# A two-head state product on VectorE: one instruction with a masked decay in place of two half-height ones

## The chip, the core and the metric

The kernel runs on one core of a Trainium2 chip. The metric is the time of one execution on the device in microseconds; what is shown is the median of several runs. The engines are TensorE (PE in the profile; PEld is its loading of weights), VectorE (DVE), ScalarE (ACT), GpSimd (POOL), and SP, which issues most DMAs.

## What is computed

A recurrent attention with a state per head (4 batches, 8 heads, 768 steps, 40 channels a head) is followed by a two-layer network with a squared ReLU. Cut to what matters:

```
for t in range(S):
    y[:, :, t] = einsum('bhd,bhde->bhe', r_t, state)
    Sa = einsum('bhde,bhe->bhd', state, a_t)
    state = state * w_t[:, :, None, :] - einsum('bhd,bhe->bhde', Sa, b_t)
    state = state + einsum('bhd,bhe->bhde', v_t, k_t)
x = y with the heads of a token side by side          # 3072 x 320
out = relu(x @ w_in) ** 2 @ w_out                     # 3072 x 2048, then 3072 x 320
```

## The kernel before

The sequence is cut into 6 chunks of 128 tokens. In a chunk the recurrence is turned into matrix products, and only the state at the chunk's end goes on to the next chunk. A chunk of one of the 4 batches is a "batch" m of the code (24 of them), prepared by `add_prep`. Its 8 heads are 4 pairs; two pairs make a "step" (`add_step`, 48 steps, two per batch). In a pair, head s = 0 has partitions 0 to 63 and head s = 1 partitions 64 to 127, with 40 of the 64 filled.

In the preparation of a batch, ScalarE turns the decays w into logarithms and exponentials, GpSimd and VectorE make the scaled keys KB and cast the rest to bf16, and TensorE or a transposing DMA turns them. The cumulative decays of the chunk end in the tile GT (5 in a ring, line 151): 128 partitions, 4 pairs, 130 columns, of which column 0 is one and columns 1 to 128 are the decays (`e_gt`); column L = 128 is the decay over the whole chunk. Batch 0 is prepared in two parts of two pairs (`o.parts`, line 253), all others in one.

A step runs through: products ca and their masking CN (line 485, DVE); the matmuls P and two corrections (lines 494 to 509) with c between them (line 522, DVE); the transposition TB, which also turns the carried state (lines 546 and 552); the products ex and their masking EVX (line 571, DVE); the matmuls of line 582 (`kb_mm`) and, from chunk 1 on, those of line 590 (`z_mm`), which leave outputs and new state together in one PSUM bank: 168 columns a pair, 128 of outputs and 40 of state. From there `ys` (line 595) writes the outputs of the step and `uz` (line 599) the state, both multiplied by decays of GT on VectorE.

`uz(u)` is called twice a step in the first five chunks (40 steps, 80 instructions), once for each head u of both pairs. Its result goes into the tile UZ of the next chunk (2 in a ring, line 153): 128 partitions, 16 pairs, 128 columns, in which head 0 has the columns 0 to 39 of its 64 partitions and head 1 the columns 64 to 103 of its own. The other two blocks of a pair must be zero, since the matmul of line 494 contracts over all 128 partitions. They are zero because `blank` (line 195) zeroes each whole tile at the start, and `uz` never writes there.

The instructions of all engines are issued in one written-out order (`ORDER`, line 835, with the engine of each movable operation in `WAYS`): `add_step` only declares operations with their costs and needs, here `("UZ", st, u)` at line 649, and a planner assigns buffers and banks while it follows the order. Each engine works its own instructions off in that order. The two products of a step stand next to each other in some places and up to five microseconds apart in others, with either head first: steps 0, 1, 3, 2 begin with head 0, steps 4, 5, 7, 9 with head 1, steps 6 and 8 with head 0. The readers of the state are the transposes of line 552, four steps or more later, and the matmuls of line 494, eight steps later. The transposes of a step, the network's matmuls (lines 723 and 760) and the rest of the step's matmuls fill TensorE in between. In the network `hs` and `Gt` (lines 731 to 742) are spread over ScalarE, VectorE and GpSimd.

Of the kernel before, what the change touches and what calls it, by code (L numbers as in the profile page):

```python
# [8 lines left out]
BF16 = mybir.dt.bfloat16  # L9
I32 = mybir.dt.int32  # L10
ALU = mybir.AluOpType
# [7 lines left out]
def kernel(  # L19
# [12 lines left out]
    nc = tc.nc  # L32

    NB, NHH, T, D = r.shape
    L = 128
    NCH = T // L
    PB = NHH // 2
# [6 lines left out]
    LV = L + D  # L44
# [4 lines left out]
    gl = ctx.enter_context(tc.tile_pool(name="gl", bufs=1))  # L49
# [30 lines left out]
    def buf(ring, kind=None):  # L80
        b_ = Buf(ring, kind)
        if ring != "bank":
            row = rings.setdefault(ring, [])
            b_.n = len(row)
            row.append(b_)
        return b_
# [58 lines left out]
    MEX = gl.tile([128, 4, L], BF16, name="MEX")  # L145
    IDs = gl.tile([128, D], BF16, name="IDs")
    MCN = gl.tile([128, 2, 2, L], BF16, name="MCN")
    banks = [ps.tile([128, 512], FP32, name=f"bank{i}") for i in range(NBANK)]
    fixed = {}
    for ring, shape in (("KB", [128, 2, NHH, 64]), ("GA", [128, 2, NHH, 64]),  # L150
                        ("RV", [128, 2, NHH, 64]), ("GT", [128, PB, L + 2]),
                        ("EVX", [128, PB, 2, EV]), ("RVT", [128, 2, PB, L]),
                        ("UZ", [128, NP, 128])):
        fixed[ring] = [gl.tile(shape, BF16, name=f"{ring}{i}") for i in range(RING[ring])]
# [5 lines left out]
        out=UTI[:], in_=ones_f[:], pattern=[[1, 128]],  # L160
# [5 lines left out]
        out=IDb[:], in_=ones_b[:], pattern=[[1, 128]],  # L166
# [6 lines left out]
    for i in range(26):  # L173
# [3 lines left out]
        out=UTb[:], in_=ones_b[:], pattern=[[1, 128]],  # L177
# [4 lines left out]
        out=MEX[:], in_=MEX[:], pattern=[[0, 4], [1, L]],  # L182
# [3 lines left out]
    def blank(ring, i):  # L186
        t_ = fixed[ring][i]
        if ring in ("KB", "GA", "RV"):
            nc.vector.memset(t_[:, :, :, D:64], 0.0)
        elif ring == "GT":  # L190
            nc.gpsimd.memset(t_[:, :, 0:1], 1.0)
        elif ring == "EVX":
            nc.gpsimd.memset(t_[:, :, :, 2 * LV:EV], 0.0)
        elif ring == "UZ":
            nc.vector.memset(t_[:], 0.0)

    for i in range(2):
        for ring in ("KB", "GA", "RV"):
            blank(ring, i)
    for u, sg in ((0, 1.0), (1, -1.0)):  # L200
        nc.vector.tensor_scalar(out=MCN[:, :, u, :], in0=MEX[:, 0:2, :],
                                scalar1=sg, scalar2=None, op0=ALU.mult)
    for i in range(2):
        for ring in ("GT", "EVX"):
            blank(ring, i)
    later = {}
    for ring, a_, b_, eng, cost in (("KB", 2, 5, "DVE", 0.21), ("UZ", 1, 2, "DVE", 1.0),
                                    ("GT", 2, 5, "POOL", 0.05), ("EVX", 2, 5, "POOL", 0.2),
                                    ("UZ", 0, 1, "DVE", 1.0)):
        for i in range(a_, b_):  # L210
            rank = i - 1.5 if ring != "UZ" else (7.0, 0.5)[i]
            later[ring, i] = ("blank", ring, i)
            op(("blank", ring, i), eng, rank, cost, cost + 0.05, [], [],
               lambda ring=ring, i=i: blank(ring, i))
# [5 lines left out]
    def half(s):  # L220
        return slice(64 * s, 64 * s + 64)
# [23 lines left out]
    for m in range(NBC):  # L245
        o = Batch()
# [9 lines left out]
    def part(m, u):  # L256
        return u if m < SPLIT else 0

    def sb(b_, shape, dtype):
        if b_.tile is None:  # L260
            pool = natp if b_.ring[0] == "N" else rot
            b_.tile = pool.tile(shape, dtype, name=b_.ring, tag=b_.ring,
                                bufs=RING[b_.ring if b_.ring in RING else "N"])
        return b_.tile
# [184 lines left out]


    SU, MERGE = 4, 12
    CNb, TBb = [buf("CN") for _ in range(NS)], [buf("TB") for _ in range(NS)]
    c1b, x1b = ([buf(x) for _ in range(NS)] for x in ("c1", "x1"))
    Mcb, Ccb = ([buf(x) for _ in range(NCH)] for x in ("Mc", "Cc"))
    UZb, YSb = [None] + [buf("UZ") for _ in range(1, NCH)], [buf("YS") for _ in range(NCH)]
# [3 lines left out]
    def add_step(st):  # L459
        c, q = divmod(st, NQ)  # L460
        m, u_ = divmod(st, 2)
        o, j0, p2, p = bt[m], 2 * u_, slice(2 * q, 2 * q + 2), part(m, u_)
        EVX = o.EVX.tile[:, j0:j0 + 2]
        UZ = UZb[c].tile if c else None
# [5 lines left out]
        def quads(b_):  # L470
            return b_.tile[:].rearrange("p (i u t) -> p i u t", i=2, u=2)
# [11 lines left out]
        def cn(s):  # L483
            t_ = sb(CN_, [128, 2, 2, 2, L], BF16)
            nc.vector.tensor_tensor(out=t_[:, :, s], in0=quads(ca[s]), in1=MCN[:], op=ALU.mult)  # L485

# [88 lines left out]
        def uy():  # L575
            return uyb.tile[:, 0:2 * LV].rearrange("p (i x) -> p i x", i=2)
# [19 lines left out]
                                    in1=o.GT.tile[:, j0:j0 + 2, 0:L], op=ALU.mult)  # L596

        def uz(u):
            nc.vector.tensor_tensor(  # L599
                out=UZb[c + 1].tile[half(u), p2, 64 * u:64 * u + D], in0=uy()[half(u), :, L:LV],  # L600
                in1=o.GT.tile[half(u), j0:j0 + 2, L:L + 1].to_broadcast([64, 2, D]), op=ALU.mult)

        op(("ca", st), "PE", st, *pe(0.225), [("KBT", m, p), ("AT", m, p)], [o.KBT, o.AT] + ca,
           ca_mm, "R")
# [25 lines left out]
        n = 512 if carry else 256  # L630
# [16 lines left out]
        if c + 1 < NCH:  # L647
            for u in range(2):
                op(("UZ", st, u), "DVE", st + 4.05, 0.15, 0.234,
                   [last, ("GT", m, p)] + cleared("UZ", c + 1), [uyb, o.GT, UZb[c + 1]],  # L650
                   lambda u=u: uz(u))
# [437 lines left out]
```

## Time and profile before

| | |
|---|---|
| median of 3 runs | 274.46 us (272.98 to 274.72) |
| the profiled execution | 272.03 us |
| its span, first to last instruction | 270.3 us |
| granted TensorE clock over the span | 0.981 |
| busy: PE, DVE | 254.8 us, 241.0 us |
| busy: ACT, POOL | 206.8 us, 186.2 us |
| products of line 599 | 80, of 219 to 247 ns (median 236) |

The profile is one execution. An engine's busy time is the time that its instructions' records cover, and records on one engine overlap: the next instruction can start before the one ahead of it has ended. The chain is the work that ended last, followed back from the last instruction, at each step to what released it or to the instruction ahead of it on the same engine. In a group of instructions stand the line, the engine, the operation, the tiles written and read, the shapes and the count; then busy us and the mean ns of one; then the idle time of the engine in front of them and what ended it. In the timeline a row has the start, the time, the engine and the same names; in brackets stands the idle time ahead of it and its releaser.

### The profile page before, as it was taken

To read this page: it belongs to the slowest core of one execution; us is meant where nothing else is said; L and a number is where in the kernel's file an instruction comes from. 1 tells how busy PE (TensorE), PEld (TensorE's weight loads), DVE (VectorE), ACT (ScalarE), POOL (GpSimd) and SP (SyncE) were. 2 spreads that over 40 slices of the span, in tenths; PEclk is the share of its full clock that TensorE was granted. 3 is DMA by queue.
4 is the path that set the end of the run, shared out by engine and by line. 5 is a ranking of instruction groups with operands and counts; after the bars stand their busy time and mean duration, and the time that the engine had idled before them with its cause. 6 is when DMAs were issued, how large, how long until landed. Compare 5 with 4: busy or idle time off the path is not lost.

```text
span 270.3 us, 10143 instructions
## 1 busy us (share of the span) xinstructions
PE 254.8 (94%) x3944; PEld 205.7 (76%) x3944; DVE 241.0 (89%) x564; ACT 206.8 (77%) x542; POOL 186.2 (69%) x313
## 2 busy tenths in 40 slices
PE   7885989799999999999999999999999999999994
PEld 6653668578888778778888778888888777778773
DVE  7785899999999999999999999999999888898382
ACT  3474778888999979888999878787888767966560
POOL 4396947896979797799978668786945574143360
PEclk9998589999999999999999999999999999999999
DMA  7999999997983995898897889998999978904002
GB/s 120 172 179 158 155 168 174 166 183 124 158 150 59 184 150 94 157 182 145 162 175 143 149 156 150 184 140 160 165 124 118 180 130 166 153 11 112 6 29 75
DMA packets 184034, 37.61 MB, mean 139 GB/s; under 512 B 178544, under 2 KB 183664, under 8 KB 183984
## 3 DMA queue, kind: packets, MB, share of 16 engines
q1 hardware_dynamic: 181328, 34.33, 75.6%
q0 software_dynamic: 2656, 2.62, 6.6%
q8 instruction: 31, 0.51, 0.8%
q14 instruction: 19, 0.16, 0.2%
HBM read 28.84 MB, written 3.93 MB: 121 GB/s over the span
## 4 chain that ended last, share of the span: by engine, by line
PE 62%; DVE 14%; DMA 6%; SPq 5%; ACT 4%; issue 4%; POOL 3%; DVEq 0%; POOLq 0%; ACTq 0%
PE bank L723 19%; PE bank L760 14%; PE bank L346 5%; SPq L272 5%; PE bank L582 5%; PE bank L477 4%; DVE CN L485 4%; PE bank L509 3%; PE bank L566 3%; DVE EVX L571 3%; PE bank L300 2%; PE bank L590 2%; DMA KBT<-KB 2%; DVE YS L595 2%; DMA NA<-in_a_dram 2%
## 5 line engine op out<-in xcount | busy, mean ns | idle before, releaser
L723 PE MATMUL bank<-YS,WIN 120*128 120x256 bf16 (+3 forms) x672 | 75.0, 257 | 0.3 <-DVE CN L485 0.3
L571 DVE TENSOR_TENSOR EVX<-bank,MEX 128x512 bf16<-128x512 f32 x96 | 63.8, 679 | 2.2 <-PE bank L566 1.7
L485 DVE TENSOR_TENSOR CN<-bank,MCN 128x512 bf16<-128x512 f32 x96 | 62.8, 679 | 2.0 <-PE bank L477 1.3
L723 PEld LDWEIGHTS <-WIN 120*128 120x128 bf16 (+1 forms) x672 | 54.6, 97 | 7.6 <-issue 0.4
L760 PE MATMUL bank<-WOUT,Gt 128*128 128x320 bf16 x384 | 58.6, 299 | 0.0
L742 POOL TENSOR_TENSOR Gt<-hs 128x512 bf16<-128x512 bf16 x38 | 39.6, 1044 | 26.6 <-ACT hs L731 14.5
L731 ACT ACTIVATE hs<-bank 128x512 bf16<-128x512 f32 x74 | 42.9, 596 | 8.2 <-PE bank L723 3.2
L760 PEld LDWEIGHTS <-Gt 128*128 128x128 bf16 x384 | 34.9, 97 | 12.4 <-issue 0.2
L534 ACT ACTIVATE junk<-CN 128x512 bf16<-128x512 bf16 x48 | 30.1, 628 | 1.5 <-DVE CN L485 1.0
L526 POOL TENSOR_TENSOR x<-Mc,c 128x160 f32<-128x160 bf16 x41 | 20.8, 510 | 13.5 <-DVE c L522 11.8
L331 POOL TENSOR_TENSOR KB<-NB,GI 128x320 bf16<-128x320 f32 (+1 forms) x22 | 18.8, 856 | 12.7 <-DMA NB<-in_b_dram 12.6
L530 POOL TENSOR_TENSOR Cc<-x,EVX 128x160 bf16<-128x160 f32 x46 | 23.3, 513 | 2.9 <-DVE EVX L236 1.4
L509 PEld LDWEIGHTS <-CN 128*128 128x128 bf16 x384 | 19.6, 97 | 5.8 <-issue 1.8
L582 PE MATMUL bank<-EVX,KB 128*64 128x168 bf16 x384 | 23.4, 245 | 0.1
L331 POOL TENSOR_TENSOR KB<-NK,GI 128x320 bf16<-128x320 f32 (+1 forms) x23 | 19.7, 858 | 5.1 <-ACT GI L321 2.7
L740 ACT ACTIVATE Gt<-hs 128x512 bf16<-128x512 bf16 x35 | 21.7, 632 | 1.2 <-DVE hs L733 1.0
L231 ACT ACTIVATE TB<-bank 128x512 bf16<-128x512 bf16 (+1 forms) x29 | 16.8, 578 | 7.2 <-PE bank L552 4.4
L477 PE MATMUL bank<-AT,KBT 64*128 64x128 bf16 x384 | 19.8, 222 | 2.1 <-ACT KBT L231 1.2
L595 DVE TENSOR_TENSOR YS<-bank,GT 128x256 bf16<-128x256 f32 x48 | 19.6, 413 | 1.3 <-PE bank L582 0.8
L733 DVE TENSOR_SCALAR hs<-bank 128x512 bf16<-128x512 f32 x22 | 14.8, 684 | 5.9 <-issue 3.9
L599 DVE TENSOR_TENSOR UZ<-bank,GT 64x80 bf16<-64x80 f32 x80 | 18.5, 234 | 1.5 <-PE bank L590 0.5
L522 DVE TENSOR_TENSOR c<-bank,Mc 128x160 bf16<-128x160 f32 x48 | 14.9, 314 | 5.4 <-PE bank L509 5.0
(113 smaller groups left out, 587.6 us busy)
## 6 DMA issues: line engine op xcount, KB each, us to landing
NW<-in_w_dram SPq DMA_DIRECT2D x24, 160.0 KB
NB<-in_b_dram SPq DMA_DIRECT2D x24, 160.0 KB
NK<-in_k_dram SPq DMA_DIRECT2D x24, 160.0 KB
NA<-in_a_dram SPq DMA_DIRECT2D x24, 160.0 KB
NV<-in_v_dram SPq DMA_DIRECT2D x24, 160.0 KB
NR<-in_r_dram SPq DMA_DIRECT2D x24, 160.0 KB
out_dram<-osb SPq DMA_DIRECT2D x24, 160.0 KB
WOUT<-in_moe_w_out_dram POOLq DMA_DIRECT2D x4, 320.0 KB, 5.6
```

The lines of the kernel that those rows point to most:

```text
L331: engine(eng).tensor_tensor(out=o.KB.tile[:, u, h, 0:D], in0=o.nat[key].tile[:, h], in1=o.GI.tile[:, h], op=ALU.mult)
L477: nc.tensor.matmul(out=quads(ca[s])[:, i, u, :], lhsT=o.KBT.tile[half(s), u, j0 + i, :], rhs=o.AT.tile[half(s), j0 + i, :], start=(i == 0 ...
L485: nc.vector.tensor_tensor(out=t_[:, :, s], in0=quads(ca[s]), in1=MCN[:], op=ALU.mult)
L509: nc.tensor.matmul(out=P[:, 2 * i + s], lhsT=CN[:, i, s, 1, :], rhs=X[:, 2 * i + s], start=False, stop=last, skip_group_check=True)
L534: nc.scalar.activation(out=t_, in_=CN_.tile[:, :, :, 1, :], func=ACTF.Square, accum_out=ACC[:, AN + st:AN + st + 1])
L571: nc.vector.tensor_tensor(out=EVX[:, :, s, 0:2 * LV].rearrange("p i (u x) -> p i u x", u=2)[:, :, :, 0:L], in0=quads(ex[s]), op=ALU.mult, ...
L582: nc.tensor.matmul(out=uy()[half(s), i, :], lhsT=o.KB.tile[:, u, 2 * (j0 + i) + s, :], rhs=EVX[:, i, s, LV * u:LV * u + LV], start=(i == 0 ...
L595: nc.vector.tensor_tensor(out=t_[:, p2, :], in0=uy()[:, :, 0:L], in1=o.GT.tile[:, j0:j0 + 2, 0:L], op=ALU.mult)
L723: nc.tensor.matmul(out=hp[:, u], lhsT=WIN[g][0:ROWS[g], j * 128:(j + 1) * 128], rhs=by_pair()[0:ROWS[g], g], start=(g == 0 and u == 0), st ...
L731: nc.scalar.activation(out=t_, in_=hpb.tile[:], func=ACTF.Relu)
L742: engine(eng).tensor_tensor(out=t_, in0=x_, in1=x_, op=ALU.mult)
L760: nc.tensor.matmul(out=opb.tile[:, 0:DM], lhsT=Gtb[h].tile[:, j, b_, :], rhs=WOUT[:, j, :], start=(j == 0), stop=(j == NJ - 1))
```

## The change

The two products of a step become one of 128 partitions. It reads the state columns of the bank once for either block of columns (a broadcast with stride zero), multiplies by a pair of decays for each pair of heads, and writes both blocks, so that the off-diagonal blocks are now written too, as zeros. The pair of decays is new: GT gets two more columns (L + 2 and L + 3), which hold the chunk's decay times a mask HM, one in the partitions of the column's own head and zero in those of the other. One tiny product on VectorE makes them for all pairs of a part of a batch, directly ahead of the first state product that reads them (21 times: batch 0 has two parts, batches 1 to 19 one). HM is filled at the start by three GpSimd fills. The zeroing of UZ at the start is confined to the 24 unused columns of each 64.

Order and costs are left as they are: both operations are still declared, and whichever comes first in the order issues the one instruction; the second issues nothing.

```
+    HM = gl.tile([128, PB, 2], BF16, name="HM")
...
-                        ("RV", [128, 2, NHH, 64]), ("GT", [128, PB, L + 2]),
+                        ("RV", [128, 2, NHH, 64]), ("GT", [128, PB, L + 4]),
...
-            nc.vector.memset(t_[:], 0.0)
+            nc.vector.memset(t_[:].rearrange("p n (s x) -> p n s x", s=2)[:, :, :, D:64], 0.0)
...
+    nc.gpsimd.memset(HM[:], 0.0)
+    for s in range(2):
+        nc.gpsimd.memset(HM[64 * s:64 * s + 64, :, s:s + 1], 1.0)
...
+    made = set()
...
         def uz(u):
+
+            if (st, "UZ") in made:
+                return
+            made.add((st, "UZ"))
+            j_, n_ = o.parts[p]
+            by = o.GT.tile[:, j_:j_ + n_, L + 2:L + 4]
+            if (m, p) not in made:
+                made.add((m, p))
+                nc.vector.tensor_tensor(out=by, in1=HM[:, 0:n_], op=ALU.mult,
+                                        in0=o.GT.tile[:, j_:j_ + n_, L:L + 1].to_broadcast([128, n_, 2]))
+            by = o.GT.tile[:, j0:j0 + 2, L + 2:L + 4].rearrange("p i (s x) -> p i s x", x=1)
             nc.vector.tensor_tensor(
-                out=UZb[c + 1].tile[half(u), p2, 64 * u:64 * u + D], in0=uy()[half(u), :, L:LV],
-                in1=o.GT.tile[half(u), j0:j0 + 2, L:L + 1].to_broadcast([64, 2, D]), op=ALU.mult)
+                out=UZb[c + 1].tile[:, p2].rearrange("p i (s x) -> p i s x", s=2)[:, :, :, 0:D],
+                in0=uy()[:, :, L:LV].rearrange("p i (s x) -> p i s x", s=1).to_broadcast([128, 2, 2, D]),
+                in1=by.to_broadcast([128, 2, 2, D]), op=ALU.mult)
```

## The prediction

> **What bounds the kernel now.** I read the page first: the busy shares, then the chain of work that ended last.
>
> ```profile
> PE 254.8 (94%) x3944; PEld 205.7 (76%) x3944; DVE 241.0 (89%) x564; ACT 206.8 (77%) x542; POOL 186.2 (69%) x313
> PE 62%; DVE 14%; DMA 6%; SPq 5%; ACT 4%; issue 4%; POOL 3%; DVEq 0%; POOLq 0%; ACTq 0%
> ```
>
> TensorE (PE) and VectorE (DVE) are both nearly full, but the chain lies on PE for 62% of the span and on DVE for only 14%, some 38 us. A share over the whole span mixes stages, so next I cut the span into windows. Each row gives the length and the busy time of PE, PEld, DVE, ACT and POOL.
>
> ```profile
> 30.00:40.00 10.00, 8.74 (x124) 6.20 (x120) 9.77 (x23) 7.51 (x17) 5.98 (x13) 0.73 0.98 161
> 40.00:50.00 10.00, 9.01 (x159) 7.42 (x160) 9.84 (x29) 8.08 (x24) 8.06 (x13) 1.00 1.13 163
> 50.00:60.00 10.00, 8.85 (x156) 6.49 (x154) 9.92 (x21) 8.55 (x23) 8.99 (x15) 1.00 1.24 187
> 60.00:75.00 15.00, 14.94 (x282) 12.93 (x279) 14.80 (x35) 13.34 (x38) 12.57 (x20) 1.00 0.80 137
> 150.00:180.00 30.00, 30.00 (x466) 24.56 (x463) 29.19 (x69) 24.43 (x71) 21.62 (x33) 1.00 0.97 160
> ```
>
> There are two regimes. From 30 to 60 us DVE is never free (29.5 of 30 us) while PE leaves 3.4 us open: this ramp is DVE's. From 60 us on PE is full too (30.00 of 30 in the last row). What DVE saves there is worth only as much as PE still stalls for it.
>
> **What the two products cost now.** The groups show the 80 products of line 599 and, for comparison, the 48 subtractions of line 522, which read as many elements from PSUM as the new product will (160 in a partition).
>
> ```profile
> L599 DVE TENSOR_TENSOR UZ<-bank,GT 64x80 bf16<-64x80 f32 x80 | 18.5, 234 | 1.5 <-PE bank L590 0.5
> L522 DVE TENSOR_TENSOR c<-bank,Mc 128x160 bf16<-128x160 f32 x48 | 14.9, 314 | 5.4 <-PE bank L509 5.0
> ```
>
> Durations overlap on DVE, so what an instruction takes from its engine is the time to the next start. DVE's timeline:
>
> ```profile
> 46.03 0.69 DVE L571 TENSOR_TENSOR EVX<-bank,MEX 128x512 bf16<-128x512 f32 x1
> 46.74 0.24 DVE L599 TENSOR_TENSOR UZ<-bank,GT 64x80 bf16<-64x80 f32 x1
> 46.99 0.42 DVE L742 TENSOR_TENSOR Gt<-hs 128x512 bf16<-128x512 bf16 x1
> ...
> 47.67 0.31 DVE L522 TENSOR_TENSOR c<-bank,Mc 128x160 bf16<-128x160 f32 x1
> 47.90 0.22 DVE L599 TENSOR_TENSOR UZ<-bank,GT 64x80 bf16<-64x80 f32 x1
> 48.05 0.41 DVE L406 TENSOR_TENSOR AT<-bank,GT 128x512 bf16<-128x512 bf16 x1
> ...
> 57.22 0.68 DVE L571 TENSOR_TENSOR EVX<-bank,MEX 128x512 bf16<-128x512 f32 x1
> 57.82 0.22 DVE L599 TENSOR_TENSOR UZ<-bank,GT 64x80 bf16<-64x80 f32 x1
> ```
>
> The products are of two kinds. The quick one starts 0.60 us after EVX (57.22 to 57.82), before EVX has ended, and the next instruction starts 0.15 us later (47.90 to 48.05). The slow one waits until EVX is over (46.03 to 46.74, 0.71 us), and the next waits until it is over (46.74 to 46.99, 0.25 us). A slow one so takes 0.11 + 0.25 = 0.36 us from DVE. Both kinds read and write 80 elements in 64 partitions; I take the slow one for the head in partitions 64 to 127, as each step has one of each. A step pays 0.15 + 0.36 = 0.51 us, and 40 steps pay 20.4 us.
>
> The Trainium skill has a rule for this ("VectorE: DVE Perf Modes", section "Two Vector instructions with no wait between them"): an instruction whose operands start in another group of 32 partitions than those of the one before is held until everything before it has finished. [...]
>
> **The change, part by part.**
>
> *The product of both heads.* 128 partitions by 160 elements, from PSUM, starting at partition 0: as line 522, whose successor starts 0.23 us later (47.67 to 47.90). The quick product already broadcasts its decay without a penalty. 40 x 0.23 = 9.2 us.
>
> *The masked decay.* 21 new tiny products (8 elements; two for batch 0, which has two parts, one for each of batches 1 to 19), and the product behind each has to wait for it on DVE itself. The nearest rows are the tiny instructions of the final check:
>
> ```profile
> 264.31 0.15 DVE L816 SCALAR_TENSOR_TENSOR ok<-es 1x12 f32<-1x12 f32 x1
> 264.39 0.17 DVE L819 TENSOR_SCALAR ok<-es 1x48 f32<-1x48 f32 x1
> 264.59 0.27 DVE L821 TENSOR_REDUCE nok<-ok 1x1 f32<-1x120 f32 x1
> 264.89 0.14 DVE L822 TENSOR_SCALAR bad<-nok 1x1 int32<-1x1 f32 x1
> ```
>
> One of 12 elements lasts 0.15 us, and a dependent successor starts 0.03 us after the end (264.86 to 264.89). I take 0.18 us, nearest by size. Ends: 0.08 us if the wait cost nothing (264.31 to 264.39), 0.30 us if it were as long as the reduction with its wait (264.59 to 264.89). 21 x 0.18 = 3.8 us. Behind it queue all later DVE instructions, such as the CN and EVX products for which PE and ScalarE wait.
>
> DVE then pays 9.2 + 3.8 = 13.0 us for 20.4: it is relieved of 7.4 us. The Trainium skill's prices speak against so much (same page, section "The TRN2 errata"): 120 cycles and one per element from PSUM, 58 and one per element from SBUF, at 0.96 GHz. An estimate by them is a relief of 40 x (0.42 - 0.29) - 21 x 0.07 = 3.7 us, and counted along the chain, as below, a gain of 0.25 us and 274.2 us; they hold no price for the wait of the slow kind, which the rows show.
>
> *What of that lies on the path.* The chain passes through products of line 599 seventeen times, first and last at 29.48 and 148.40:
>
> ```profile
> 29.48 0.14 DVE UZ L599
> ...
> 45.28 0.24 DVE UZ L599
> ...
> 72.35 0.24 DVE UZ L599
> ...
> 124.52 0.14 DVE UZ L599
> ...
> 148.40 0.20 DVE UZ L599
> ```
>
> That path remains, with new lengths, so its loss is about the most that can be won. The merged product stands where the first of the two stood. By stretches on DVE, old against new, with 0.09 to 0.11 us of hold ahead of each slow one:
> - 29 to 37 us: steps 0, 1 and 3, each the first of its part, so each pays 0.18 + 0.23. Old 0.66 for three products by 31.3 and 0.53 for two by 36.3, new 3 x 0.41 = 1.23: loss 0.04.
> - 43.8 to 54.6: step 2's slow product goes (its merged one stands at 40.28, off the chain); step 4 has one decay. At 47.43 the gain is 0.37 + 0.37 - 0.41 = 0.33. Step 4's quick one and step 5 would give 0.44 more, but next late is another row:
>
> ```profile
> 49.64 0.62 PE L346 MATMUL bank<-IDb,KB 128*128 128x128 bf16 x8 [0.47 <-POOL KB L331]
> ```
>
> PE waits there for GpSimd's KB, and EVX at 50.63 waits for PE. I leave the 0.44 out and keep it for the range: 0.33.
> - 57.0 to 62.6: step 6 with a decay (0.41), step 7 without (0.23), for 0.15 + 0.37 + 0.37: 0.25.
> - 70.5 to 75.1: step 9 without: 0.35 + 0.15 - 0.23 = 0.27.
> - 110.6, 124.5 and 147.8 to 148.6: 0.35 - 0.23 = 0.12; 0.49 - 0.41 = 0.08; 0.35 + 0.15 - 0.23 = 0.27.
>
> Sum: 1.28 us. The other 6 us are slack that PE, full after 60 us, doesn't take.
>
> *Edits with one answer: nothing.* The zeroing of UZ covers 24 of 64 columns instead of all, two instructions of 912 ns now, perhaps 0.4 us after. They run at 4.3 and 6.9 us, when the chain lies on SP's issues of loads and then on a load:
>
> ```profile
> 14.47 4.09 DMA NA<-in_a_dram
> ```
>
> The three fills of the mask stand ahead of GpSimd's first multiplication, before which it idles anyway; uncovered they would cost what three fills of 0.12 us cost:
>
> ```profile
> 6.49 0.65 POOL L331 TENSOR_TENSOR KB<-NK,GI 128x160 bf16<-128x160 f32 x1 [2.68 <-ACT GI L321]
> ```
>
> GT's rows grow by two columns: same elements, same instructions. The product that moves forward needs the same matmuls as its twin, so there is no new wait on PE; the transposes and matmuls that read the state come steps later. No DMA moves and no queue of SP is passed.
>
> **The rivals.**
> - *Relief for PE everywhere* (faster): DVE is at 97% even from 150 to 180 us, so small PE stalls inside busy time might shrink too. If half of the 7.4 us came through, 274.46 - 3.7 = 270.8. Against it: PE at 30.00 of 30, and that of the chain's 38 us on DVE only 12 lie after 75 us (27 pieces, the first and the last):
>
> ```profile
> 82.96 0.42 DVE GT L234
> ...
> 205.96 0.61 DVE hs L733
> ```
>
> - *Hidden altogether*: the tiny product and the second half now stand ahead of CN and EVX at the earlier place (0.26 us later there), and the gain at the later place finds PE or GpSimd late, as at 49.64. Sum zero: 274.5.
> - *The hold stays* (slower): if the slow kind were slow for its wait and not for its partitions, each merged product would cost 0.11 + 0.25 + 0.08 (80 more elements) = 0.44 us instead of 0.23. With 11 on the chain that is 2.3 us more: 274.46 - 1.28 + 2.3 = 275.5. It decides above 0.51 - 0.09 = 0.42 us a product (0.09 is a step's half of the decay). Against it: the quick kind waits for the same matmuls and isn't held.
>
> **How the numbers follow.** Gain on the chain only: chance 0.57; hidden: 0.17; relief everywhere: 0.13; the hold stays: 0.13. The profiled execution took 272.03 us around a span of 270.3; less 1.28 it is 270.75. The median of the runs is 2.43 us above it (274.46), and the same difference gives 273.2. The likeliest's own range: six decays lie on the chain, 0.10 less each gives 0.6 more, with the 0.44 left out 272.1; 0.12 more each gives 273.9. For 8 in 10 the range is carried towards the two outer rivals until about half of each is inside: 271.3 to 275.6, which leaves out some 0.15. About 1% (2.7 us) is what a measurement here tells from no change. Faster by more means under 271.7, most of the relief rival: 0.13. Slower by more means above 277.2; the hold with decays at 0.30 us makes 276.2, so it takes new PE stalls as well: 0.08. Within 1%: 0.79.
>
> **What would show it.** Line 599: 40 products of 128x160 near 314 ns with successors 0.23 us later, and no 0.71 us after an EVX in front of them: the hold is gone. 0.44 us there: the third rival. A group of 21 tiny products near 0.15 us, the product starting 0.18 us after each; much more makes the wait the story. DVE's busy time falls by some 6 us and its idle grows after 60 us, while PE's busy time stays; if PE's windows from 60 to 250 us shorten as well, the relief was wider. I am wrong if the tiny product's wait, a later PE clock in 30 to 40 us (0.73 now) or a load that comes late decides instead.

## The result, and the profile after

The changed kernel takes 273.73 us (median of 21 runs, 271.31 to 277.28) and the kernel before 272.98 us beside it (21 runs, 269.58 to 276.32). The ratio is 1.0051, with a 95% interval of 1.0027 to 1.0076: half a per cent slower, where half a per cent faster was forecast. The two medians give 1.0027, so the size of the loss is uncertain; the forecast gain is absent by either. Ratios here and below leave out disturbed runs, those over 1.5% above the fastest of their kernel, so a single quick run of the kernel before can raise a ratio: beside e5 to e8 one of 269.15 us leaves 12 of its 29 runs, and for these four experiments the quotient of the plain medians is given as well. The profiled execution of the changed kernel, 277.28 us, is the longest of its 21.

The page after, busy times and the chain by engine:

```profile
PE 256.5 (93%) x3944; PEld 207.7 (75%) x3944; DVE 238.3 (86%) x545; ACT 206.8 (75%) x542; POOL 186.2 (68%) x316
PE 67%; DVE 10%; DMA 8%; SPq 5%; ACT 3%; issue 3%; POOL 2%; DVEq 0%; POOLq 0%; ACTq 0%
```

DVE is relieved (241.0 to 238.3 us busy), but by less than half of the 6 us that the prediction named. The two kinds of product that took the place of line 599, by shape:

```profile
L615 DVE TENSOR_TENSOR UZ<-bank,GT 128x160 bf16<-128x160 f32 x40 | 12.6, 320 | 2.1 <-PE bank L595 0.3
L612 DVE TENSOR_TENSOR GT<-GT,HM 128x8 bf16<-128x8 bf16 x19 | 5.8, 306 | 0.0
L612 DVE TENSOR_TENSOR GT<-GT,HM 128x4 bf16<-128x4 bf16 x2 | 1.5, 766 | 0.0
```

The merged product is as forecast (320 ns for 314). The tiny one is not: 7.3 us for 21, where 0.15 us each had been taken, 3.2 us. Size is not the reason, since the smaller shape has the longer mean. DVE's timeline where the ramp begins:

```profile
29.48 0.42 DVE L600 TENSOR_TENSOR YS<-bank,GT 128x256 bf16<-128x256 f32 x1 [0.56 <-PE bank L587]
29.82 0.15 DVE L612 TENSOR_TENSOR GT<-GT,HM 128x4 bf16<-128x4 bf16 x1
30.01 0.33 DVE L615 TENSOR_TENSOR UZ<-bank,GT 128x160 bf16<-128x160 f32 x1
30.25 1.28 DVE L490 TENSOR_TENSOR CN<-bank,MCN 128x512 bf16<-128x512 f32 x2
31.45 1.38 DVE L612 TENSOR_TENSOR GT<-GT,HM 128x4 bf16<-128x4 bf16 x1
32.86 0.32 DVE L615 TENSOR_TENSOR UZ<-bank,GT 128x160 bf16<-128x160 f32 x1
```

The first tiny product takes 0.15 us and the state product starts 0.19 us after it, as forecast. The second, of the same shape, takes 1.38 us. GpSimd's timeline over the same stretch:

```profile
28.79 1.50 POOL L697 DMA_DIRECT2D WIN<-in_moe_w_in_dram  x3
30.29 0.46 POOL L238 CAST RV<-NV 128x320 bf16<-128x320 f32 x1
30.71 0.86 POOL L335 TENSOR_TENSOR KB<-NB,GI 128x320 bf16<-128x320 f32 x1
31.52 0.44 POOL L238 CAST RV<-NR 128x320 bf16<-128x320 f32 x1
31.93 0.48 POOL L531 TENSOR_TENSOR x<-Mc,c 128x160 f32<-128x160 bf16 x1
32.36 0.44 POOL L238 CAST EVX<-NV 128x320 bf16<-128x320 f32 x1
33.56 0.49 POOL L535 TENSOR_TENSOR Cc<-x,EVX 128x160 bf16<-128x160 f32 x1 [0.76 <-ACT GT L235]
```

The quick one ran while GpSimd issued DMAs (28.79 to 30.29). The slow one starts while GpSimd multiplies KB, waits through three more instructions that follow each other without a gap, and ends at 32.83, 0.03 us after the last of them (32.36 + 0.44 = 32.80), when GpSimd falls idle. And it lies on the chain:

```profile
30.34 1.19 DVE CN L490 x2
31.53 1.30 DVE GT L612
```

The Trainium skill has a rule for this that the prediction did not weigh ("SBUF — State Buffer", section "SBUF: two separate sides"): VectorE and GpSimd share a second pair of SBUF ports under an exclusive lock, which VectorE needs for an instruction with two SBUF inputs or in a two-port mode; whoever starts first has it for the whole instruction, and the other waits. The rows agree with a wait to the end of GpSimd's work; here the loser waited for more than one instruction. Elsewhere in the same profile it got its turn between two of them (VectorE, then GpSimd):

```profile
80.03 0.47 DVE L612 TENSOR_TENSOR GT<-GT,HM 128x8 bf16<-128x8 bf16 x1
80.03 0.45 POOL L238 CAST RV<-NR 128x320 bf16<-128x320 f32 x1
80.44 0.72 POOL L308 TENSOR_TENSOR r<-lnW 128x320 f32<-128x320 f32 x1
```

This one ends at 80.50, 0.02 us after the cast, while GpSimd's next instruction is already running. Why it lost several times in a row in the ramp, no run here shows.

It could have been read from the kernel before. Two groups of its profile, both with two operands in SBUF, have means well above what their quick members take (the x at 57.97 takes 0.31 us, the Gt at 46.99 0.42 us):

```profile
L742 DVE TENSOR_TENSOR Gt<-hs 128x512 bf16<-128x512 bf16 x23 | 12.3, 540 | 0.8 <-ACT hs L731 0.8
L526 DVE TENSOR_TENSOR x<-Mc,c 128x160 f32<-128x160 bf16 x7 | 4.2, 606 | 0.1
```

The windows of the ramp after:

```profile
30.00:40.00 10.00, 6.58 (x98) 5.00 (x98) 9.06 (x21) 6.33 (x16) 5.32 (x11) 0.79 0.90 154
40.00:50.00 10.00, 9.64 (x137) 7.98 (x138) 8.41 (x19) 7.39 (x19) 7.22 (x13) 0.69 1.05 151
```

From 30 to 40 us PE issues 98 matmuls where it issued 124, though its granted clock there is no lower (0.79 for 0.73). The clock of 0.69 from 40 to 50 us, where it was 1.00 before, is not shown to come from the change: the place of such a dip differs between executions of like kernels, as the part on the bound below shows.

### The profile page after: what moved, and what is told of

It reads as the page before. It is cut to its first block, busy times and chain, and to the rows that moved or that the text cites. A ratio compares the mean times of both kernels' runs of the same rounds, so it can differ in the third digit from the quotient of the medians.

```text
span 275.6 us, 10136 instructions
## 1 busy us (share of the span) xinstructions
PE 256.5 (93%) x3944; PEld 207.7 (75%) x3944; DVE 238.3 (86%) x545; ACT 206.8 (75%) x542; POOL 186.2 (68%) x316
## 4 chain that ended last, share of the span: by engine, by line
PE 67%; DVE 10%; DMA 8%; SPq 5%; ACT 3%; issue 3%; POOL 2%; DVEq 0%; POOLq 0%; ACTq 0%
PE bank L740 19%; PE bank L777 14%; PE bank L350 7%; PE bank L587 5%; SPq L276 5%; PE bank L482 4%; PE bank L514 3%; PE bank L571 3%; PE bank L304 3%; DMA NA<-in_a_dram 3%; DMA WOUT<-in_moe_w_out_dram 2%; PE bank L595 2%; PE bank L551 2%; DVE EVX L576 2%; DMA KBT<-KB 2%
## 5 line engine op out<-in xcount | busy, mean ns | idle before, releaser
L740 PE MATMUL bank<-YS,WIN 120*128 120x256 bf16 (+3 forms) x672 | 76.1, 260 | 0.7 <-DVE YS L600 0.7
L740 PEld LDWEIGHTS <-WIN 120*128 120x128 bf16 (+1 forms) x672 | 55.6, 99 | 7.9 <-issue 0.8
L308 POOL TENSOR_TENSOR r<-lnW 128x320 f32<-128x320 f32 x21 | 15.2, 725 | 7.8 <-ACT lnW L290 3.8
L587 PEld LDWEIGHTS <-KB 128*64 128x64 bf16 x384 | 14.7, 112 | 6.1 <-issue 3.2
```

What stands on the lines that cost most here:

```text
L587: nc.tensor.matmul(out=uy()[half(s), i, :], lhsT=o.KB.tile[:, u, 2 * (j0 + i) + s, :], rhs=EVX[:, i, s, LV * u:LV * u + LV], start=(i == 0 ...
L740: nc.tensor.matmul(out=hp[:, u], lhsT=WIN[g][0:ROWS[g], j * 128:(j + 1) * 128], rhs=by_pair()[0:ROWS[g], g], start=(g == 0 and u == 0), st ...
```

## The experiments

Theory P (port): the tiny product waits for GpSimd, and that is what turned the gain into a loss. Rival W (wait): what costs is that the state product has to wait for a result of its own engine. Rival M (move): the second half, moved forward, delays work that is needed earlier. Each ratio is to the kernel before on the same chip. Lines of code left out are marked "...".

**e1, the changed kernel again.** No edit.

> The changed kernel once more, for a second profile and a second measure. Theory P (port): the tiny product on VectorE reads two operands from SBUF and waits until GpSimd's running instruction is over, so the 21 of them take some 9 us of VectorE and not 3.8; expects the ratio to the kernel before at 1.002 to 1.008 again, and in the profile tiny products of 0.15 us where GpSimd is idle or issues DMAs and of 0.3 to 1.4 us where it computes, each ending some 0.02 us after a GpSimd instruction. Rival W (wait): the tiny product is 0.15 us whatever GpSimd does and the product's wait for it is what costs; expects constant 0.15 us and long gaps behind. Rival M (move): the second head's half now stands ahead of work that is needed earlier, whatever the tiny product costs; expects the tiny product's time to be beside the point.

Measured: 1.0007 (0.9963 to 1.0052), below P's range, and too wide to tell the changed kernel from the one before; the 21 runs above are the better measure. The profile has P's picture, with a worse case at another place. DVE:

```profile
29.66 2.60 DVE L612 TENSOR_TENSOR GT<-GT,HM 128x4 bf16<-128x4 bf16 x1
32.28 0.33 DVE L615 TENSOR_TENSOR UZ<-bank,GT 128x160 bf16<-128x160 f32 x1
32.53 1.28 DVE L490 TENSOR_TENSOR CN<-bank,MCN 128x512 bf16<-128x512 f32 x2
33.72 0.15 DVE L612 TENSOR_TENSOR GT<-GT,HM 128x4 bf16<-128x4 bf16 x1
```

GpSimd, first and last of five instructions without a gap:

```profile
29.73 0.46 POOL L238 CAST RV<-NV 128x320 bf16<-128x320 f32 x1
...
31.79 0.44 POOL L238 CAST EVX<-NV 128x320 bf16<-128x320 f32 x1
```

This time the first tiny product met the row of five and waited 2.6 us, until 32.26, again 0.03 us after the last; the second found GpSimd free. Which of them is hit depends on some tenths of a microsecond. That fits W badly: its constant 0.15 us is not there.

**e2, without the tiny product.** The mask alone is the factor, filled with 2^-20 in place of 1, so the decay of the state over a chunk is left out:

```
-            by = o.GT.tile[:, j_:j_ + n_, L + 2:L + 4]
-            if (m, p) not in made:
...
-            by = o.GT.tile[:, j0:j0 + 2, L + 2:L + 4].rearrange("p i (s x) -> p i s x", x=1)
+            by = HM[:, 0:2].rearrange("p i (s x) -> p i s x", x=1)
```

> The changed kernel without the tiny product: the state is multiplied by the mask alone (a constant in the size of the decays), so the decay of the state over a chunk is left out; everything else stays. P and W expect VectorE relieved of 20.4 - 9.2 = 11 us and the chain without six decays: 1.28 + 6 x 0.18 = 2.4 us less, a ratio of 0.991 (0.987 to 0.996). M expects no gain: 1.000 to 1.005.

Measured: 0.9867 (0.9794 to 0.994). All else that the change does is a gain of about 1.3%, measured in six runs, and M, which expected none, falls.

**e3 and e12, the masked decays from PSUM.** They are made behind AT, some microseconds ahead, from the bank that AT reads:

```
+                if not a_d:
+                    nc.vector.tensor_tensor(
+                        out=o.GT.tile[:, j0:j0 + n, L + 2:L + 4], in1=HM[:, 0:n], op=ALU.mult,
+                        in0=bank(b1)[:, 0:n * L].rearrange("p (j t) -> p j t", t=L)[
+                            :, :, L - 1:L].to_broadcast([128, n, 2]))
```

> The masked decays are made right behind the product AT of the same batch, from the bank in PSUM that AT reads, so that the tiny product has one operand in SBUF only and nothing waits for it at once. P expects 21 tiny products that take 0.1 us each, none stretched by GpSimd, and a ratio of 0.992 to 0.997. W expects the same time. M expects 1.000 to 1.006.

> The masked decays from PSUM behind AT once more, beside these three on one chip: expected at 0.990 to 0.997 again, with tiny products of 0.15 us and 0.07 us to the next start.

Measured: 0.9941 (0.9898 to 0.9985), and again 0.9938 (0.9899 to 0.9976). None is stretched, and what follows mostly starts 0.08 us later (e3, the group and one in the timeline):

```profile
L415 DVE TENSOR_TENSOR GT<-bank,HM 128x8 bf16<-128x8 bf16 x19 | 3.0, 155 | 0.0
```

```profile
35.37 0.16 DVE L415 TENSOR_TENSOR GT<-bank,HM 128x8 bf16<-128x8 bf16 x1
35.45 0.32 DVE L532 TENSOR_TENSOR c<-bank,Mc 128x160 bf16<-128x160 f32 x1
```

**e4, the tiny product alone.** The kernel before, with both halves, and the 21 tiny products in their places:

```
         def uz(u):
+            if (m, p) not in made:
+                made.add((m, p))
+                ...
+                nc.vector.tensor_tensor(out=o.GT.tile[:, j_:j_ + n_, L + 2:L + 4], in1=HM[:, 0:n_], op=ALU.mult, ...)
             nc.vector.tensor_tensor(
                 out=UZb[c + 1].tile[half(u), p2, 64 * u:64 * u + D], ...
```

> The kernel before with the wider GT and the 21 tiny products in the places of the changed kernel, their results unused; the two products of a step stay as they were. P expects tiny products of 0.15 to 1.4 us, 7 to 9 us in all on VectorE, and, with eight or so of them on the chain, a ratio of 1.008 to 1.02. W expects 21 x 0.08 us and a ratio of 1.000 to 1.004, as nothing waits for them. M expects 1.000.

Measured: 1.0135 (1.0072 to 1.0197), with a mean of 270 ns for the tiny products, 5.7 us in all. Alone and with nobody waiting for them, they cost the kernel more than 0.7%. W expected at most 0.4%.

**e5, the tiny product early, but from SBUF.** As e3, with `in0=o.GT.tile[:, j0:j0 + n, L:L + 1]`.

> The tiny product of the changed kernel, both operands from SBUF as there, but right behind the product AT of its batch, some microseconds before the state product that reads it: the wait for it is gone, the port is still asked for. P expects tiny products of 0.15 us up to over 1 us again, 5 to 9 us in all, and a ratio between the masked decays from PSUM (0.994) and the changed kernel (1.003): 0.997 to 1.006. W expects them at 0.15 us and the ratio at 0.994.

Measured: 1.006 (1.0029 to 1.0091), and 0.999 by the medians (273.17 to 273.37 us). By the medians e3 had 0.991, on another chip; e7 below, from PSUM and on the same chip as e5, took 270.36 us, so e5 is 1.0% longer (its state products stand earlier than those of e7). In its edit the one operand in SBUF instead of PSUM is the whole difference to e3, and the stretched products are back:

```profile
L415 DVE TENSOR_TENSOR GT<-GT,HM 128x8 bf16<-128x8 bf16 x19 | 5.7, 302 | 0.0
```

**e9, at the old place, with the wait, but from PSUM.** The converse of e5; the first operand is the state bank, and the mask is filled with 2^-40 in place of 1, so the decays mean nothing:

```
-                                        in0=o.GT.tile[:, j_:j_ + n_, L:L + 1].to_broadcast([128, n_, 2]))
+                                        in0=uyb.tile[:, 0:n_].rearrange("p (i x) -> p i x", x=1).to_broadcast([128, n_, 2]))
```

> The tiny product at the place of the changed kernel and with the same wait behind it, but with the state bank in PSUM as its first operand in place of GT (so the decays are numbers without meaning, scaled down by the mask; nothing else is left out). Only the mask comes from SBUF. P expects 21 tiny products of 0.15 us each, none stretched by GpSimd, the state product 0.18 to 0.25 us behind each, and a ratio of 0.992 to 0.999. W, for which the wait behind it is the cost, expects the changed kernel's 1.002 to 1.008.

Measured: 0.9936 (0.99 to 0.9972). The row of GpSimd instructions is there too, and the tiny product runs right into it (DVE, then GpSimd):

```profile
30.64 0.15 DVE L612 TENSOR_TENSOR GT<-bank,HM 128x4 bf16<-128x4 f32 x1
30.82 0.33 DVE L615 TENSOR_TENSOR UZ<-bank,GT 128x160 bf16<-128x160 f32 x1
```

```profile
30.42 0.86 POOL L335 TENSOR_TENSOR KB<-NB,GI 128x320 bf16<-128x320 f32 x1
```

It starts inside GpSimd's KB and ends inside it. The wait is in place and costs 0.18 us to the next start, the price that had been forecast. With e5 this decides for P: neither the place nor the wait makes the loss.

**e6, one tensor operand from SBUF instead of two.** The mask becomes a scalar of each partition, which takes two instructions:

```
+                for s in range(2):
+                    nc.vector.tensor_scalar(out=by[:, :, s:s + 1], in0=o.GT.tile[:, j_:j_ + n_, L:L + 1],
+                                            scalar1=HMf[:, s:s + 1], scalar2=None, op0=ALU.mult)
```

> At the place of the changed kernel, with the same wait behind, but with the mask as a scalar of each partition in place of the second operand: two tiny instructions a part (one for each head), each with a single tensor read from SBUF. P expects each at 0.15 us whatever GpSimd does, some 0.3 us from the first to the state product, 6 us in all, and a ratio of 0.995 to 1.000. W expects no gain over the changed kernel, as the wait is there and an instruction more: 1.003 to 1.008.

Measured: 1.025 (1.0199 to 1.0301), and 1.017 by the medians (278.04 to 273.37 us), the worst of all by either, and against both forecasts:

```profile
L613 DVE TENSOR_SCALAR GT<-GT,HMf 128x4 bf16<-128x4 bf16 x38 | 13.5, 410 | 0.0
```

The shortest of them takes 218 ns. One pair, and GpSimd beside it:

```profile
127.02 1.18 DVE L613 TENSOR_SCALAR GT<-GT,HMf 128x4 bf16<-128x4 bf16 x2
127.13 1.03 POOL L760 TENSOR_TENSOR Gt<-hs 128x512 bf16<-128x512 bf16 x1
```

The pair ends at 128.20, 0.04 us after GpSimd's instruction. P was worded too narrowly. A bf16 instruction of VectorE with a single tensor read from SBUF and a scalar per partition waits as well, and there are twice as many of them. What the stopped ones have in common here is not two tensors; it is that no tensor input comes from PSUM. The Trainium skill's rule on the shared pair ("SBUF — State Buffer", section "SBUF: two separate sides") covers it by its other clause, the two-port modes; which clause applies to these instructions no run here shows.

**e7, at the later place.** e3, with the state product where the second of the two stood:

```
-            if (st, "UZ") in made:
-                return
-            made.add((st, "UZ"))
+            if (st, "UZ") not in made:
+                made.add((st, "UZ"))
+                return
```

> As the masked decays from PSUM (ratio 0.994), but the state product of a step stands where the second of the two stood, not the first. M, in the weak form that the earlier place costs something, expects 0.988 to 0.992. P alone expects the same within the noise: 0.991 to 0.997.

Measured: 0.9945 (0.9899 to 0.9991), the same as e3, but 0.989 by the medians (270.36 to 273.37 us). The first is what P alone expected and the second lies in the range of M's weak form, so it stays open whether the later place gains something more. It can't be what turned the gain into a loss, since e3 and e9 keep the earlier place and gain.

**e8, the tiny product on GpSimd.** `nc.gpsimd.tensor_tensor`, issued in `ex_ev` of the first step of a part.

> The tiny product goes to GpSimd, issued with the masking EVX of the first step of its part, so VectorE carries none and the state product waits for GpSimd. P expects VectorE's ramp from 29 to 38 us as without the tiny product, and a ratio of 0.988 to 0.996, unless GpSimd reaches it late; then waits of the state product for GpSimd show in the profile and the ratio is 0.996 to 1.003. M expects 1.000 to 1.005.

Measured: 1.0046 (0.9998 to 1.0093), and 0.996 by the medians (272.24 to 273.37 us). The two point in opposite ways; the run decides nothing.

**e10, both halves at partition 0.** The kernel before with `half(0)` for `half(u)` in the product, so the second head's state is left out. It tests the step of the prediction that the slow kind is slow for its partitions.

> The kernel before with both products of a step on partitions 0 to 63 (the state of the second head is left out, that of the first is written to both blocks). If the slow kind of product is slow for starting at partition 64, all 80 take 0.15 us to the next start, the 0.71 us after EVX are gone, VectorE is relieved of some 8 us without a tiny product, and the ratio is 0.985 to 0.995. If the slow kind is slow for its place or its waits, 40 of them stay slow and the ratio is 0.998 to 1.002.

Measured: 0.994 (0.9898 to 0.9982), and all products are of the quick kind (mean 223 ns, before 234; none is longer than 234 ns, where the slow ones before took up to 247):

```profile
L599 DVE TENSOR_TENSOR UZ<-bank,GT 64x80 bf16<-64x80 f32 x80 | 16.8, 223 | 0.7 <-PE bank L590 0.6
```

With the same number of instructions in the same order, the partition alone is worth 0.6%.

**e11, the layout.** The wider GT and the mask, unused.

> The kernel before with the wider GT and the three fills of the mask, neither of them used. All theories expect no difference: 0.997 to 1.003; if GT's row length of 132 in place of 130 columns costs or gains anything, it shows here, in the mean times of AT and YS.

Measured: 1.0025 (0.9983 to 1.0067); AT takes 415 ns for 414 and YS 415 for 413. No effect that can be told from none.

## Why the prediction was wrong

- *What bounds the kernel*: right as far as the runs show. What VectorE saves or loses reaches the end in part (e2 and e10 gain, e4 loses); no run changes the ramp alone.
- *The two kinds of product and the hold*: right, and shown by e10. 128x160 takes 320 ns for 314, and the next start follows after 0.24 us (30.01 to 30.25) for the 0.23 forecast. The hold also works the other way round: on the chain before, step 5 begins with its slow product at 49.45, and the one of partition 0 right behind it starts only at 49.72, when the slow one is over.
- *The masked decay*: this is the step that failed. It was priced at 0.18 us, with 0.30 as the upper end, from the tiny instructions of lines 816 to 822. Those rows come from the last microseconds, where GpSimd has nothing left to do; over the kernel GpSimd is busy for 186.2 of 270.3 us. The 21 took 7.3 us, and with the 2.1 us that VectorE idles ahead of the merged products, nearly all of it behind a tiny one, some 9.4 us, not 3.8: 0.45 each, beyond the upper end. Of the excess some 4.1 us are the stretch (7.3 less 21 x 0.15), the rest is that idle time. The chain of the changed kernel passes through six of them, the two in the ramp and four later:

```profile
80.11 0.40 DVE GT L612
...
90.87 0.38 DVE GT L612
...
111.61 0.19 DVE GT L612
...
134.18 0.34 DVE GT L612
```

  The six have 2.69 us on the chain (with 1.30 at 31.53, as above, and 0.08 at 29.91), and 3.13 us to the starts of the products behind them, where 6 x 0.18 = 1.08 had been forecast. The 2.05 us more are above the gain of 1.28 and leave a loss of about 0.8 us; 1.4 us were measured by the ratio (0.7 to 2.1), 0.75 by the medians. The largest part of it is the one in the ramp (1.38 us here, 2.60 in e1). That six were forecast and six are found is partly luck: only the two in the ramp are among the prediction's. And this is one execution, so the sum shows the size of the loss and not its exact amount. The shape was taken as what makes a row near; where its operands lie, and what GpSimd does at the time, should have been.
- *The bound that the chain gives*: it fits as far as it can be tested. With a tiny product of 0.08 us it gives 1.28 + 6 x 0.10 = 1.9 us, and e3 and e12 won 1.6 and 1.7. Without the tiny product it gives 2.4 us; e2 won 1.3%, some 3.6 us, with an interval of 1.6 to 5.6. The granted clock may have a part in that. From 30 to 40 us it was 0.73 before, and e3 has:

```profile
30.00:40.00 10.00, 8.00 (x145) 6.00 (x146) 10.00 (x25) 8.61 (x20) 6.52 (x15) 1.00 1.00 160
```

  But e11, which does the same work as the kernel before in the same time, has 0.98 there in its own profile, and 0.85 from 40 to 50 us, where the kernel before had 1.00:

```profile
30.00:40.00 10.00, 7.23 (x128) 5.44 (x128) 9.77 (x25) 7.89 (x17) 6.30 (x14) 0.98 0.89 145
40.00:50.00 10.00, 9.42 (x148) 7.95 (x144) 8.95 (x25) 7.47 (x23) 7.60 (x13) 0.85 1.02 159
```

  So the place of the dip differs between executions of like kernels, and what it adds to e2's gain stays open. A later clock, which the prediction named as a sign of being wrong, does not explain the missing gain: over the whole span it was 0.984 in the mean of e1's 12 runs of the changed kernel, and 0.982 in the 23 of the kernel before beside them.
- *The number*: 273.73 us lies half a microsecond from the forecast 273.2, and that is luck. The forecast stood on a kernel before of 274.46 us (3 runs), which took 272.98 us in 21.
- *The rivals*: the one that ended on the slower side had the wrong mechanism (the hold that stays; e10 and the rows after show that it goes). "Hidden altogether" does not fit e2, e3 and e10, which gain. Relief for PE everywhere does not fit e12: its tiny products mostly take 0.08 us to the next start, so VectorE is relieved of some 9.5 us (20.4 - 9.2 - 1.7), of which half would be 4.7 us; the gain is 1.7 us (0.7 to 2.8).
- *Edits costed at nothing*: right, as far as e11 shows for GT's rows and the fills. The smaller zeroing of UZ was not tried alone.

The version that beats both kernels is e3: the change as it is, with the masked decays from PSUM. It stands at 0.994 to the kernel before in both measurements, and beside e1 it took 271.98 us where the changed kernel took 274.59. e7, the same at the later place, may be as good or better.

## What to carry to other kernels

A tiny instruction on VectorE is not cheap by its size. Before one is added, look where its operands lie: if all of them are in SBUF and GpSimd computes at the time, it can wait for GpSimd, as here, and everything behind it waits too, so let one operand come from PSUM, or issue it where GpSimd is idle. A group whose mean lies well above its shortest member in the profile before is the sign to look for, and two products that start at different partitions are worth merging for the hold alone.

## What the runs showed of the hardware that had not been expected

- VectorE can lose to GpSimd several times in a row: five GpSimd instructions without a gap kept one product of 4 elements a partition waiting for 2.60 us (e1).
- A product on VectorE with one operand in PSUM and one in SBUF is not stopped: in e9 it started and ended inside a GpSimd instruction, and the 21 took 148 to 168 ns.
- An instruction with a single SBUF tensor and a scalar per partition is stopped as well (e6: mean 410 ns over 38, the shortest 218 ns).
